# An opening and a first maxout group in one hand-fixed order on every engine, early reads of the second group's blocks, and weights joined in two VectorE operations

## The chip, the cores and the metric

One Trainium2 chip, one core of it. A time is the device time of one execution in microseconds (us), and a kernel's time is the median of its executions in the runs named. All executions told of here were in the fast state, so no slow run had to be set aside. A span is the profiled execution from its first to its last instruction; it is 1 to 3 us shorter than the time.

## The reference, cut to what matters

```python
# delta rule: q, k, v are (4, 8, 768, 48), beta is (4, 8, 768)
k_n = k / (np.linalg.norm(k, axis=-1, keepdims=True) + 1e-06)
for t in range(S):
    y[:, :, t] = einsum('bhd,bhde->bhe', q_t, state)
    v_old      = einsum('bhde,bhd->bhe', state, k_t)
    state      = state + b_t * einsum('bhd,bhe->bhde', k_t, v_t - v_old)
x = y.transpose(0, 2, 1, 3).reshape(3072, 384)
# maxout layer with d_ff = 768
h = np.maximum(np.maximum(x @ w1, x @ w2), x @ w3)
out = h @ w_out
```

The kernel takes the delta rule in chunks of 64 steps, twelve chunks, two to a *group*, six groups. A chunk needs the inverse of a small triangular matrix for every batch and head. Group m's inverses are computed by `solve(m)`: 31 steps of elimination on VectorE, each one multiplication and one subtraction that need the step before. Then come joins and products on TensorE, which end in the group's x, and the maxout layer `ffn(m)` of the group: 6 hidden tiles of 3 products and 2 maxima each (in the first group 9, as three of them are done in two halves), and 4 output tiles.

Some names recur. A *unit* is one chunk for half of the batch, so a group has four. `turn` transposes a unit's k or q, and `gram` forms its products; the one that involves q is then multiplied by a triangular mask (the *mask product*). The other goes to DRAM, and its diagonal blocks are read back by `blocks(m)`; they are what `solve(m)` works on. z, u, y and x are the chain after the solve, in this order, and each needs a product on TensorE and a copy (this y is the delta rule's output; the solve's own result is called y as well, `y_bl` in the lines). The *norm* is the scaling of k to unit length.

## The kernel before: the parts that the argument touches

The solve is a serial chain on VectorE. Each engine works through a queue of its own, and an operation that waits at its head holds what stands behind it (an instance below: a copy that was ready to run stood 7.1 us behind two others).

```python
def solve(m):
    x = xs[m]                               # the blocks, read back from DRAM by blocks(m)
    y = work.tile([128, BL, BL], FP32, name="y_bl", bufs=1)
    nc.gpsimd.memset(y, 0.0)
    norm(bl, ...)                           # sqrt on ACT, five small operations on DVE
    ...
    for j in range(BL - 1):                 # "the loop"
        nc.vector.tensor_tensor(out=t_v, in0=x[...], in1=y[...], op=ALU.mult)
        nc.vector.tensor_tensor(out=y[...], in0=y[...], in1=t_v, op=ALU.subtract)
        yield
    # y goes out to DRAM and comes back transposed, as ut2, t1 and ut
    nc.vector.tensor_copy(x[0:32]...., y[0:32])      # staged in x itself
    nc.scalar.copy(x[32:64]...., y[32:64])
```

A piece of the weights (24 in all) is put together from its two halves over three engines: ACT shifts, VectorE takes a sign off, POOL clamps, VectorE does two more operations, POOL adds. The order of only two engines is fixed by hand, SyncE (which issues transfers) and ScalarE, and in the opening alone; a scheduler orders the rest.

```python
with tc.manual_schedule(engines={SP, Activation}):
    ... loads, turn(0..3), gram(0..3) ...
    blocks(0)
    some(conv, 2)                # two pieces of the weights
    some(solving, 32)            # solve(0)
    ... turn(4..7), gram(4..7) ...
    blocks(1)
    join_z(0); some(conv, 1); join_u(0); old_k(0); old_q(0); new(0); to_y(0); to_x(0)
solving = solve(1)
for m in range(GROUPS):
    for i, _ in enumerate(ffn(m)):      # links of the next group's chain between the tiles
        ...
        if i == SOLVE - 2: blocks(m + 2)
        if i == SOLVE:     solving = solve(m + 2)
```

## Time and profile before

| | before |
|---|---|
| median of 3 runs | 623.84 us |
| span | 622.2 us |
| PE busy, of the span | 544.3 us, 87% |
| DVE, ACT, POOL busy | 51%, 25%, 14% |

The shares of a whole span hide the story; the prediction below cuts the span into stretches. Two waits of TensorE between the end of solve(0) and the first group, 52.4 to 74.3, are worth a look because the argument comes back to them (columns: us in total, times, longest):

```profile
PE p_z L447 <- DMA ut<-y_d: 9.0, 2, 8.5
...
PE p_j L466 <- POOL w_sb L216: 3.3, 1, 3.3
```

The first is the way of y through DRAM. The second is a wait put down to weights: the z products were done, but their copy stood in ScalarE's and VectorE's queues.

### The profile page before, as it was taken

The numbers are of one execution on the slowest core, as the hardware profiler recorded it, in microseconds if no ns is written. First come the engines' busy times: TensorE is split into PE (matmuls) and PEld (weight loads), VectorE is DVE, ScalarE is ACT, GpSimd is POOL, SyncE is SP. The second block draws the span as 40 slices with busy tenths as digits, with TensorE's granted clock in tenths as the row PEclk, the third lists the DMA queues.
The fourth block names the chain that finished last, engine by engine and source line by source line (L and its number), as shares of the span: only waits on it lengthen the run. The fifth ranks groups of instructions, "written<-read, shape, count | busy, mean of one in ns | idle before, by whom it ended". The sixth has DMA issues, their size and how long they took to land.

```text
span 622.2 us, 17590 instructions
## 1 busy us (share of the span) xinstructions
PE 544.3 (87%) x7718; PEld 324.9 (52%) x7718; DVE 317.6 (51%) x748; ACT 153.5 (25%) x255; POOL 87.3 (14%) x123
## 2 busy tenths in 40 slices
PE   5361786676799999999999999999999999999997
PEld 4251675452555554655655545555555555554444
DVE  0797159998364982369722499132596222101110
ACT  4333222323421232221332121432112120110001
POOL 7102204445141002000110000200000100000000
PEclk9656599887799999999999999999999999999999
DMA  9775813553771544352355321542103400020002
GB/s 196 141 162 123 184 34 110 137 112 72 205 124 20 108 99 91 79 95 52 77 111 98 65 52 27 106 91 44 36 1 79 77 2 3 3 49 1 0 0 51
DMA packets 158412, 48.47 MB, mean 78 GB/s; under 512 B 143296, under 2 KB 153344, under 8 KB 158336
## 3 DMA queue, kind: packets, MB, share of 16 engines
q1 hardware_dynamic: 156096, 46.87, 36.3%
q8 instruction: 60, 0.98, 0.7%
q10 hardware_dynamic: 2112, 0.39, 0.4%
q14 instruction: 16, 0.13, 0.1%
q0 software_dynamic: 128, 0.10, 0.1%
HBM read 31.56 MB, written 15.73 MB: 76 GB/s over the span
## 4 chain that ended last, share of the span: by engine, by line
PE 66%; DVE 23%; issue 4%; ACT 2%; DMA 2%; POOL 1%; SPq 0%; POOLq 0%; ACTq 0%; DVEq 0%
PE p_h L591 39%; PE p_o L615 11%; DVE tmp L376 7%; DVE y_bl L382 7%; PE p_t L285 3%; PE p_g L307 3%; PE p_u L516 2%; PE p_s L534 2%; PE p_k L488 2%; PE p_y L551 1%; PE p_q L488 1%; PE p_z L447 1%; DVE h L601 1%; PE p_j L466 1%; DVE mant L208 1%
## 5 line engine op out<-in xcount | busy, mean ns | idle before, releaser
L591 PE MATMUL p_h<-xt,w_sb 128*128 128x512 f32 (+1 forms) x702 | 301.4, 578 | 18.8 <-POOL w_sb L216 7.2
L591 PEld LDWEIGHTS p_h<-xt,w_sb 128*128 128x128 f32 x702 | 131.3, 195 | 145.6 <-issue 117.2
L601 DVE TENSOR_TENSOR h<-h,p_h 128x512 f32<-128x512 f32 (+1 forms) x78 | 50.2, 644 | 148.5 <-PE p_h L591 147.3
L615 PE MATMUL p_o<-wo_sb,h 128*128 128x384 f32 x288 | 96.5, 489 | 1.6 <-DVE h L601 1.5
L615 PEld LDWEIGHTS p_o<-wo_sb,h 128*128 128x128 f32 x288 | 53.6, 190 | 39.7 <-DVE h L601 4.6
L376 DVE TENSOR_TENSOR tmp<-x_bl,y_bl 128x31 f32<-128x31 f32 (+15 forms) x186 | 69.2, 372 | 4.9
L382 DVE TENSOR_TENSOR y_bl<-y_bl,tmp 128x31 f32<-128x31 f32 (+15 forms) x186 | 65.8, 354 | 4.6
L599 ACT COPY h<-p_h 128x512 f32<-128x512 f32 (+1 forms) x39 | 21.6, 553 | 129.7 <-PE p_h L591 129.7
L258 POOL TENSOR_TENSOR v_t<-v_t,nrm 128x768 f32<-128x768 f32 x12 | 17.8, 1482 | 175.1 <-DMA v_t<-in_v_dram 51.1
L307 PE MATMUL p_g<-kqt 64*64 64x64 f32 (+1 forms) x1280 | 33.4, 250 | 8.4 <-ACT kqt L291 7.1
L307 PEld LDWEIGHTS p_g<-kqt 64*64 64x64 f32 x1280 | 28.3, 149 | 16.8 <-ACT kqt L291 10.0
L291 ACT COPY kqt<-p_t 128x1024 f32<-128x1024 f32 (+1 forms) x28 | 24.6, 890 | 28.6 <-PE p_t L285 28.5
L285 PE MATMUL p_t<-ident,kpad 128*128 128x128 f32 x96 | 19.1, 333 | 11.5 <-DMA kpad<-in_k_dram 11.5
L623 ACT COPY o_sb<-p_o 128x384 f32<-128x384 f32 x24 | 11.5, 479 | 67.6 <-PE p_o L615 64.5
L203 POOL TENSOR_SCALAR mant<-mant 128x384 f32<-128x384 f32 x24 | 14.4, 600 | 82.7 <-DVE mant L199 57.7
L540 DVE TENSOR_TENSOR st<-st,p_s 128x768 f32<-128x768 f32 x11 | 10.5, 951 | 28.3 <-PE p_s L534 28.3
L456 POOL COPY ut<-ut 32x512 f32<-32x512 f32 x24 | 14.6, 608 | 72.9 <-DMA ut<-y_d 71.9
L285 PE MATMUL p_t<-ident,qpad 128*128 128x128 f32 x96 | 17.7, 313 | 7.1 <-DMA qpad<-in_q_dram 5.2
L447 PE MATMUL p_z<-ut,at 64*32 64x32 f32 x768 | 10.8, 203 | 14.8 <-DMA ut<-y_d 14.8
L317 DVE TENSOR_TENSOR pt<-p_g,mask 128x512 f32<-128x512 f32 x24 | 16.4, 687 | 11.2 <-PE p_g L307 11.1
L216 POOL TENSOR_TENSOR w_sb<-mant,up 128x384 int32<-128x384 int32 x18 | 18.8, 1045 | 23.9 <-DVE mant L212 12.7
L325 ACT COPY at<-p_g 128x512 f32<-128x512 f32 x24 | 14.0, 585 | 32.1 <-DVE pt L317 26.6
(74 smaller groups left out, 444.6 us busy)
## 6 DMA issues: line engine op xcount, KB each, us to landing
w_bits<-in_moe_w_dram SPq DMA_DIRECT2D x18, 384.0 KB, 4.3
at_d<-at SPq DMA_DIRECT2D x48, 128.0 KB, 3.2
qpad<-in_q_dram SPq DMA_DIRECT2D x48, 96.0 KB, 3.4
v_t<-in_v_dram SPq DMA_DIRECT2D x24, 192.0 KB, 4.3
out_dram<-o_sb SPq DMA_DIRECT2D x48, 96.0 KB, 2.2
kpad<-in_k_dram SPq DMA_DIRECT2D x44, 96.0 KB, 3.1
x_bl<-at_d SPq DMA_DIRECT2D x24, 128.0 KB, 3.1
y_d<-y_bl SPq DMA_DIRECT2D x12, 256.0 KB, 3.5
```

The costliest lines, as they stand in the source:

```text
L216: nc.gpsimd.tensor_tensor(out=dst.bitcast(I32), in0=mant_v.bitcast(I32), in1=up_v, op=ALU.add)
L258: nc.gpsimd.tensor_tensor(out=vts[c], in0=vts[c], in1=nrm[:, :, :, None].to_broadcast([128, 2, H, D]), op=ALU.mult,)
L285: nc.tensor.transpose(p_t[:, i, j * 128 : (j + 1) * 128], src[:, 2 * j : 2 * j + 2], ident,)
L291: nc.scalar.copy(kqt.rearrange("p j b i t -> p i (j b) t")[:, some], p_t.rearrange("p i (x t) -> p i x t", t=C)[:, some],)
L307: nc.tensor.matmul(p_g[rows(bb ^ (g * i)), par, c0 : c0 + C * (1 + whole)], kq[:, 0], kq if whole else kq[:, i],)
L376: nc.vector.tensor_tensor(out=t_v, in0=x[:, j, None, j + 1 :].to_broadcast([128, a, b]), in1=y[:, 0:a, j, None].to_broadcast([128, a, b]), ...
L382: nc.vector.tensor_tensor(out=y[:, 0:a, j + 1 :], in0=y[:, 0:a, j + 1 :], in1=t_v, op=ALU.subtract,)
L488: nc.tensor.matmul(p_b[rows(bb), par, c0 : c0 + D], kqt[g][rows(par), j, bb ^ g, i], st[rows(par), bb ^ g, g, j],)
L591: nc.tensor.matmul(p_h, w_sb[i][:, t, f * 128 : (f + 1) * 128], xt[:, t, lo : lo + w], start=(t == 0), stop=(t == KT - 1),)
L599: nc.scalar.copy(h, p_h)
L601: nc.vector.tensor_tensor(out=h, in0=h, in1=p_h, op=ALU.max)
L615: nc.tensor.matmul(p_o, hs[f][:, i * 128 : (i + 1) * 128], wo_sb[:, f], start=(f == 0), stop=(f == FT - 1),)
```

## The change

Its intent: fix the order of all engines by hand in the opening and the first group; start the first blocks' reads earlier and on two queues; warm TensorE's clock up; move squares, masks and scalings off the critical engines; read the second group's blocks (`blocks(1)`) while the first solve's result is still on its way, so that `solve(1)` has its data when the first group starts; and take one VectorE operation out of every weight piece. The core of the diff, with cuts marked:

```diff
-    with tc.manual_schedule(engines={SP, Activation}):
+    by_hand.enter_context(tc.manual_schedule())          # all engines, to the end of ffn(0)
 # weights
-            nc.scalar.mul(up_v, low, 2.0**-29)
-            nc.vector.tensor_scalar(out=mant_v, in0=high, scalar1=0x7FFFFFFF, op0=bitwise_and)
+            nc.scalar.activation(out=mant_v, in_=high, func=Abs)
 ...                                                     # POOL clamps
+            nc.scalar.mul(up_v, low, 2.0**-29)
+            if waiting: joined(*waiting)                     # a piece's second half one call later
 ...
 # opening
+    busy(8, ident, ident)                                # warm-up products
+        gram(n, (0,), two_queues, nc.vector.tensor_copy) # two_queues = (nc.sync, nc.gpsimd)
+    sums_0 = first_squares(); first_norms(*sums_0)
+    some(conv, 1)
+    blocks(0, two_queues)
+    some(conv, 1)
 ...
+    zeros(st, *ut2, *t1, *ut, *zs)                       # before: at the very start
 ...
+        gram(n, (1,), soft=True)                         # mask product on POOL, not on VectorE
+    some(solving, 31)
+    x_t = next(solving)                                  # y staged in another buffer; blocks(1) here
+    busy(8, ident[0:32], x_t...)
+    for _ in range(3): some(conv, 1); fetch()
+    join_z(0); join_u(0); next(solving)
+    some(conv, 1); ...; new(0); some(conv, 1); to_y(0); to_x(0)
     solving = solve(1)
 # first group: tables say what goes between which products
+    FIRST = {0: "s0", 1: "z1 V3", ..., 30: "K14 n5 p9"}
+    CONVERT = (0, 3, 6, 9, 11, ...);  STEPS = (1, 1, 1, 2, ...)
+        if i == 29: blocks(2)
 # second group
+            if m == 1 and i == 0: solving = solve(2)     # before: inside the first group
```

> **What bounds the kernel now.** I read the page's slices first, then cut the span at the places where the work changes, then asked who TensorE waits for, then read single instructions in order of time.
>
> ```profile
> PE   5361786676799999999999999999999999999997
> ...
> DVE  0797159998364982369722499132596222101110
> ...
> PEclk9656599887799999999999999999999999999999
> ```
>
> A digit is 15.6 us. From the twelfth on TensorE is at 9 and its clock is full; before that it is at half or less, with a clock down to half. So the span splits at about 171 us, and a new order can gain only ahead of that. The cuts: solve(0) starts at 28.7 and ends at 52.4, the first maxout group starts at 74.3, solve(1) ends at 145.5, the second group starts at 213.9, the third at 302.7. Columns: stretch, then length and busy time (with instruction count) of PE, weight load, DVE, ACT, POOL, then clock, DMA share, GB/s.
>
> ```profile
> 0.00:28.70 28.70, 14.05 (x292) 10.58 (x292) 10.91 (x24) 11.06 (x21) 14.38 (x38) 0.85 0.92 175
> 28.70:52.40 23.70, 10.88 (x156) 8.81 (x156) 21.60 (x65) 7.70 (x13) 0.00 (x0) 0.57 0.69 147
> 52.40:74.30 21.90, 9.62 (x295) 8.30 (x295) 9.12 (x23) 7.93 (x11) 9.22 (x11) 0.50 0.68 140
> 74.30:94.90 20.60, 17.44 (x604) 14.25 (x600) 9.49 (x21) 4.81 (x10) 1.89 (x2) 0.91 0.34 74
> 94.90:145.50 50.60, 32.84 (x364) 25.34 (x365) 49.99 (x125) 12.52 (x24) 23.30 (x27) 0.91 0.45 110
> 145.50:171.00 25.50, 18.18 (x444) 12.19 (x443) 11.89 (x23) 11.30 (x17) 7.83 (x11) 0.78 0.69 168
> 171.00:213.90 42.90, 42.90 (x550) 24.87 (x551) 28.77 (x73) 9.42 (x19) 9.21 (x10) 1.00 0.44 83
> 213.90:302.70 88.80, 87.08 (x1291) 50.30 (x1290) 58.54 (x152) 24.23 (x41) 7.85 (x8) 1.00 0.42 82
> ```
>
> Four limits stand one after the other: DMA latency to 28.7; a serial DVE loop to 52.4 (DVE 21.6 of 23.7); a chain of small steps over all engines to 74.3, no engine above 45%; then DVE, 49.99 of 50.6 us, to 145.5. After that TensorE rules. The waits of TensorE up to 172 us name the same things:
>
> ```profile
> PE p_z L447 <- DMA ut<-y_d: 13.4, 3, 8.5
> PE p_t L285 <- DMA kpad<-in_k_dram: 11.5, 4, 4.6
> PE p_h L591 <- POOL w_sb L216: 7.2, 3, 3.8
> ```
>
> Columns: us in total, times, longest. And single instructions (start, duration):
>
> ```profile
> 52.12 0.21 DVE L382 TENSOR_TENSOR y_bl<-y_bl,tmp 128x31 f32<-128x31 f32 x1
> ...
> 121.25 1.01 POOL L216 TENSOR_TENSOR w_sb<-mant,up 128x384 int32<-128x384 int32 x1 [1.55 <-DVE mant L212]
> 121.33 1.15 DVE L199 TENSOR_SCALAR mant<-w_bits 128x384 uint32<-128x384 uint32 x1
> ```
>
> The last line is the one to see: the same DVE operation takes 0.34 us at 53.24, and 1.15 us here, where it starts just after a POOL addition and ends with it.
>
> **What the Trainium skill says.** (1) "TensorE: Matmul & The Clock Gate", Part 1: an idle TensorE runs at half clock and needs about 3.4 us of sustained work to get the full one. The trace agrees: 0.50 in 52.4 to 74.3, 1.00 after 171; four transposes take 1.08 us in the first and 0.6 us warm. (2) "SBUF — State Buffer", section "SBUF: two separate sides": VectorE and GpSimd share a port pair that one of them holds for a whole instruction while the other blocks. The two lines above agree. (3) "DMA: Bandwidth & Descriptors", "Issuing engines are not separate DMA queues": a second issuing engine saves only the issue time. In this trace that time is not small: four reads of the first blocks take 4.25 us on SP. But the only transfers issued by GpSimd (beta) have a median of 5.4 us to landing, against 3.1 for the block reads. (4) "ScalarE: Activation LUTs", "Table sets": cheap functions, abs among them, are in every table set. The trace has one table load (1.28 us, at 3.62), with copy, square and sqrt in use; so I expect Abs on ACT to add none.
>
> **The change part by part.**
>
> *Loads to solve(0).* Before, the last copy of the first products ends at 12.84; its transfer out waits behind others (issues until 15.2), the reads run on one queue from 16.96 to 21.2, and the first use (sqrt of the diagonal) is at 23.94. After: eight warm-up matmuls, copies on DVE beside those on ACT, two issuing queues, and the q loads moved behind. Four transposes and copies shortened by about 0.5 us each give 2 us, two queues another 2 of the 4.25; the GpSimd half lands later (5.4 against 3.1 us) and gives 1 back: 3 us earlier, solve starts at 25.7. The two sums of squares (one 0.54 us reduce lies in the loop) move out of it. But POOL, idle (0.00) in the loop before, now gets two v scalings of 1.48 us and four mask products (estimated 1.3 us from its 1.0 us for 384 columns): 8.2 us, each of which can hold up a loop operation of two SBUF operands. I take a quarter, 2 us. Loop 23.7 - 0.5 + 2 = 25.2: it ends at 51, 1.4 us earlier.
>
> *solve(0) to the first group, 21.9 us before.* Writing y out and reading it back was 52.33 to 57.5, the second half 58.4; it stays, 6 us. Then z waited until 62.07 for squares in the ACT queue: these are gone, about 3 us. The clock is warm: two joins, two products and six transposes of 1.1, 1.1, 2.0, 2.0 and 1.5 us become 0.7, 0.7, 1.1, 1.1 and 0.8: 3.3 us. Three copies of 0.8 us split over two engines save about 0.3 each: 0.9. Given back: DVE and POOL have three weight pieces in their queues ahead of the z copy, and POOL also issues t1 reads there: I take 1.3. So 16 us, and the first group starts at 67.
>
> *First group up to the end of solve(1), 71.2 us before.* x of the second group is there at once, and solve(1) starts at 67; before it did at 89.8 and took 55.7 us. DVE's work in this part: solve 23 + 4 of setup; 13 pieces x (0.35 + 0.55) = 11.7 (before 0.35 more each); maxima 12 x 0.41 + 2 x 0.69 = 6.3; chunk 1 (two st of 0.95, z 0.69, v 0.95, ut 0.69, y 0.95) 5.2; two norms 4.4. Sum 54.7. Instructions ready at once overlap by 0.08 us in the records, some 80 of them: -6. Stretching by POOL: of 23.3 us POOL in the DVE-bound stretch before I count some 11 us as lost to DVE; with one operation less per piece to be hit and a hand order I take 8. So 57 us. TensorE's own work is less: 18 x 1.49 + 3 x 2.68 for the hidden layer, 8.4 for chunk 1, 4.6 for transposes and products: 48. DVE still sets the pace; solve(1) ends at 124.
>
> *Rest of the first group, 68.4 us before.* TensorE: 6 x 2.68 + 4 x 3.9 = 31.7; chunks 2 and 3, 14.9; transposes and products of the third group, 6: 52.6. Latency of y to the second z was 157.2 - 145.5 = 11.7 us, with only some 7 us of matmuls placed before it: 5 us idle. 57.5 us; the second group starts at 181.5 instead of 213.9.
>
> *Second group.* 88.8 before. Two mask products move in (1.1), and solve(2), which had begun at 195, now begins with the group while its z stands after eight steps (26 us of TensorE against some 32 + 6 of chain). The scheduler may fill that, so 2 us in all: 90.8. From the third group on 622.2 - 302.7 = 319.5, unchanged: TensorE is at 86 of 87 to 89 us per group.
>
> Sum: 67 + 57 + 57.5 + 90.8 + 319.5 = 591.8 us of span; the time is 1.6 above the span before (623.84 against 622.2), so **593.4 us**, 4.9% less.
>
> **The rivals.** (A) TensorE-bound first group: the hand order hides all of DVE. The group then takes its matmul work, 48 + 52.6 = 101 us, and the time is 580. For it: 30% fewer DVE instructions per piece; against it: DVE at 49.99 of 50.6, and a queue in order can't slip an operation past a blocked one. (B) Head-of-line waits and POOL: in a fixed order a DVE operation that waits for POOL stops all behind it; with POOL at 8.2 us in the first loop and at some 30 in the group, twice the stretching I took costs 2 + 8 us, and GpSimd-issued transfers on the path 3: 606. For it: the 1.15 us line. (C) The gain moves into the second group: solve(2) late, z waits, TensorE idle by the whole 12 us that I mostly let the scheduler fill: 603. For it: its start moved from the first group into the second; against: all of the group's own matmuls are independent of z. (D) A transfer hides all of the opening's gain: 600.
>
> **Range and chances.** A alone gives 580, with a better opening 576; B and C together come to some 610. So 577 to 608 for 8 in 10. 2% is 611.4: faster by over 2%, 0.93; within, 0.06; slower, 0.01.
>
> **What would show it.** Right: first maxout matmul near 67; the loop of solve(0) some 25 us with POOL busy in it; clock near full from the z join on; DVE nearly full from 67 to 124; an idle stretch of TensorE of some 5 us after solve(1); groups from the third on still 87 to 89 us; one table load. Wrong: a first maxout matmul at 74 (D); DVE with gaps and TensorE full in the first group (A); DVE operations of over 1 us all through (B); idle TensorE in the second group (C).

## The result, and the profile after

The changed kernel takes 657.65 us (median of 4 runs, 655.84 to 659.44) against 623.11 of the kernel before in the same rounds. The ratio is 1.0554, 95% interval 1.0513 to 1.0595: slower, by 5.5%, where 4.9% faster was predicted. Ratios here and below are the mean time of one kernel's fast runs over that of the other's of the same rounds, so not quite the ratio of the medians quoted. The changed kernel is correct.

The same marks as in the prediction, in the profiled executions. A loop is said to start when the last multiplication of its setup ends; where other work comes in between, its first step runs up to 2 us later, and in one run 10 us later, as said there.

| mark (us) | before | predicted | after |
|---|---|---|---|
| loop of solve(0) starts | 28.7 | 25.7 | 32.5 |
| it ends | 52.4 | 51 | 61.0 |
| first maxout product | 74.3 | 67 | 87.4 |
| loop of solve(1) ends | 145.5 | 124 | 165.4 |
| second group starts | 213.9 | 181.5 | 222.4 |
| third group starts | 302.7 | 272.3 | 331.5 |
| end of the span | 622.2 | 591.8 | 654.8 |

The slices after, to lay beside those of before in the prediction (a slice is now 16.4 us):

```profile
PE   5173389655799967989989999899999999999997
...
DVE  3697377977541379433971337942359622201110
...
PEclk9567579988899979999979999999999999999999
```

TensorE's nines no longer begin at the twelfth slice and stay: a dip stands at the 15th and 16th, inside the second group, and the clock falls there and again in the 21st. The stretches (columns as in the prediction: length; busy time and instructions of PE, weight load, DVE, ACT, POOL; clock, DMA share, GB/s):

```profile
0.00:32.60 32.60, 10.81 (x187) 9.32 (x190) 14.93 (x26) 8.65 (x18) 18.85 (x44) 0.70 1.09 185
32.60:61.20 28.60, 14.91 (x292) 11.79 (x287) 26.45 (x63) 10.69 (x16) 6.84 (x5) 0.74 0.40 80
61.20:87.40 26.20, 12.86 (x278) 11.00 (x278) 10.21 (x17) 9.10 (x17) 12.63 (x18) 0.50 0.82 176
87.40:165.40 78.00, 57.89 (x792) 39.96 (x793) 64.28 (x130) 24.70 (x51) 31.80 (x34) 0.87 0.40 96
165.40:222.40 57.00, 52.67 (x1198) 34.38 (x1196) 20.70 (x34) 20.62 (x35) 11.86 (x15) 0.96 0.49 104
222.40:331.50 109.10, 93.93 (x1392) 52.41 (x1386) 70.29 (x181) 26.38 (x48) 9.51 (x9) 0.96 0.36 69
```

Every stretch but the fifth is longer than predicted. In the fourth VectorE is busy for 64.28 of 78 us, so it is not the full engine that the prediction counted on; in the last, TensorE stands idle for 109.10 - 93.93 = 15.2 us. Two waits of TensorE over the whole execution name places:

```profile
PE p_h L663 <- DVE h L674: 23.1, 9, 6.9
...
PE p_j L531 <- ACT z L517: 7.8, 1, 7.8
```

### The profile page after: what moved, and what is told of

The parts are those of the page before. It is cut to its first block, busy times and chain, and to the rows that moved or that the text cites. A ratio compares the mean times of both kernels' runs of the same rounds, so it can differ in the third digit from the quotient of the medians.

```text
span 654.8 us, 17792 instructions
## 1 busy us (share of the span) xinstructions
PE 557.5 (85%) x7818; PEld 330.2 (50%) x7818; DVE 329.0 (50%) x719; ACT 164.5 (25%) x282; POOL 105.1 (16%) x142
## 4 chain that ended last, share of the span: by engine, by line
PE 63%; DVE 17%; issue 4%; DMA 3%; ACT 2%; POOL 1%; SPq 1%; ACTq 0%; DVEq 0%; POOLq 0%
PE p_h L663 37%; PE p_o L688 10%; DVE tmp L429 5%; DVE y_bl L435 5%; PE p_g L353 2%; PE p_u L581 2%; PE p_t L331 2%; PE p_s L599 2%; PE p_k L553 1%; PE p_q L553 1%; PE p_y L616 1%; DVE mant L229 1%; DVE h L674 1%; PE p_z L512 1%; DMA ksum<-kflip 1%
## 5 line engine op out<-in xcount | busy, mean ns | idle before, releaser
L663 PE MATMUL p_h<-xt,w_sb 128*128 128x512 f32 (+1 forms) x702 | 308.6, 589 | 34.9 <-DVE h L674 23.1
L435 DVE TENSOR_TENSOR y_bl<-y_bl,tmp 128x31 f32<-128x31 f32 (+15 forms) x186 | 75.8, 407 | 5.3
L429 DVE TENSOR_TENSOR tmp<-x_bl,y_bl 128x31 f32<-128x31 f32 (+15 forms) x186 | 71.7, 386 | 5.0
L353 PE MATMUL p_g<-kqt 64*64 64x64 f32 (+1 forms) x1344 | 31.5, 238 | 16.8 <-ACT kqt L337 16.8
L353 PEld LDWEIGHTS p_g<-kqt 64*64 64x64 f32 x1344 | 26.7, 142 | 24.4 <-ACT kqt L337 20.3
L337 ACT COPY kqt<-p_t 128x1024 f32<-128x1024 f32 (+1 forms) x28 | 24.5, 889 | 14.6 <-PE p_t L331 14.6
L521 POOL COPY ut<-ut 32x512 f32<-32x512 f32 x24 | 14.6, 608 | 69.9 <-DMA ut<-y_d 68.9
L233 POOL TENSOR_TENSOR w_sb<-mant,up 128x384 int32<-128x384 int32 x18 | 18.9, 1051 | 10.4 <-DVE mant L229 10.4
L621 DVE TENSOR_TENSOR y<-qs,p_y 128x768 f32<-128x768 f32 x11 | 10.5, 951 | 19.5 <-PE p_y L616 19.5
L206 ACT ACTIVATE mant<-w_bits 128x384 f32<-128x384 f32 x24 | 13.2, 549 | 26.7 <-POOL w_sb L233 20.6
L646 ACT COPY u<-p_u 128x768 f32<-128x768 f32 x11 | 8.8, 800 | 39.1 <-PE p_u L581 39.1
L378 ACT COPY at<-p_g 128x512 f32<-128x512 f32 x20 | 11.6, 586 | 27.1 <-DVE pt L370 23.9
L518 DVE COPY z<-p_z 32x512 f32<-32x512 f32 x12 | 8.2, 688 | 20.4 <-ACT z L517 20.3
```

The source lines that it names most:

```text
L233: nc.gpsimd.tensor_tensor(out=dst.bitcast(I32), in0=mant_v.bitcast(I32), in1=up_v, op=ALU.add)
L337: nc.scalar.copy(kqt.rearrange("p j b i t -> p i (j b) t")[:, some], p_t.rearrange("p i (x t) -> p i x t", t=C)[:, some],)
L353: nc.tensor.matmul(p_g[rows(bb ^ (g * i)), par, c0 : c0 + C * (1 + whole)], kq[:, 0], kq if whole else kq[:, i],)
L429: nc.vector.tensor_tensor(out=t_v, in0=x[:, j, None, j + 1 :].to_broadcast([128, a, b]), in1=y[:, 0:a, j, None].to_broadcast([128, a, b]), ...
L435: nc.vector.tensor_tensor(out=y[:, 0:a, j + 1 :], in0=y[:, 0:a, j + 1 :], in1=t_v, op=ALU.subtract,)
L521: nc.gpsimd.tensor_copy(ut[c % NU][low, :, :, BL:C], ut2[c % NU][low])
```

## The experiments

Five causes were on the table after a first reading of the two traces, and most runs test one or two of them:

1. *Zeros.* POOL's memsets, moved to just ahead of the solve, hold VectorE.
2. *Masks.* The mask products, now on POOL, hold the loop of solve(0), and perhaps the group as well.
3. *Weights.* Weight pieces stand ahead of the z copy.
4. *Hand order.* A fixed order on VectorE, POOL and TensorE stops ready work behind work that waits.
5. *solve(2).* It starts late and runs inside the second group.

Each runs against a rival: that the cause is real in the trace but hidden behind something else, so that its removal moves no time. The kernel before measured between 623.2 and 624.5 us in the rounds of all batches, while the four runs of one variant lie up to 6 us apart; differences of medians of 1 or 2 us are not read as effects. The expectations were written batch by batch, each knowing only the runs before it; the changed kernel is called "after" in some. They are told here by cause, not in the order in which they ran.

### Zeros ahead of the solve

These lines of the changed kernel are at the start of solve(0) (start, duration, engine, line, operation, and in square brackets how long the engine had been idle and what ended that):

```profile
24.97 3.04 DVE L241 TENSOR_SCALAR nt_bl<-root_bl 128x32 f32<-128x32 f32 x1 [5.54 <-ACT root_bl L240]
25.65 1.85 POOL L92 MEMSET ut<- 128x1024 f32 x2
27.44 1.02 POOL L92 MEMSET z<- 128x512 f32 x2
...
28.43 1.55 DVE L243 TENSOR_TENSOR nt_bl<-nt_bl,x_bl 128x32 f32<-128x32 f32 x1
28.43 1.46 POOL L272 TENSOR_TENSOR v_t<-v_t,nrm 128x768 f32<-128x768 f32 x1
```

A VectorE operation on 32 elements a partition takes 3.04 us while POOL's memsets run one after another; the same operation takes 0.18 us elsewhere. The second one, 0.21 elsewhere, ends with a scaling of v on POOL. `zeros_early` puts all memsets where they were, at the start, and the loads of beta, which are also issued by POOL, behind the first products (not in the cut):

```diff
+    zeros(*(t[:, :, D:DP] for t in qpad + kpad[4:]))
+    zeros(st, *ut2, *t1, *ut, *zs)
     fetch(); fetch()
 ...
-    zeros(...)   # both calls, between blocks(0) and the loop
```

> One edit to the changed kernel: all memsets stand ahead of the first products in POOL's queue (as before the change), the beta loads behind the first products. Theory P: a DVE operation of 32 columns took 3.04 us (0.18 elsewhere) because POOL's 6.6 us of memsets, back to back, lay on the port just then; and the next one 1.55 against 0.21. The loop of solve(0) then starts at about 29 instead of 32.5, and 3 to 4 us come off the time: 653. Rival (DVE waited for the block data, not for POOL): the loop starts within 1 us of 32.5, 656 to 658.

Measured: 651.79 us, ratio 1.0453 (1.0431 to 1.0475). The two operations are short again,

```profile
24.01 0.18 DVE L241 TENSOR_SCALAR nt_bl<-root_bl 128x32 f32<-128x32 f32 x1 [4.93 <-ACT root_bl L240]
...
24.62 0.21 DVE L243 TENSOR_TENSOR nt_bl<-nt_bl,x_bl 128x32 f32<-128x32 f32 x1
```

the loop starts at 27.4 instead of 32.5, and 5.1 us at the start are worth 5.9 at the end. This cause is shown: 4.2 of the 5.1 us lie between the square root's end and the loop, where the two operations are, and 1.0 in an earlier square root.

It leaves a question: the square root before these lines starts at 24.7 in the changed kernel, and at 23.9 in the kernel before, although SyncE issues the first reads 3.6 us earlier. The other half of the reads is POOL's:

```profile
13.32 1.07 SPq L397 DMA_DIRECT2D x_bl<-at_d  x2
...
17.30 0.50 POOL L210 TENSOR_SCALAR mant<-mant 128x384 f32<-128x384 f32 x1 [4.62 <-ACT mant L206]
17.94 1.82 POOL L397 DMA_DIRECT2D x_bl<-at_d  x2
```

A weight piece stands ahead of the two issues in POOL's queue and waits 4.62 us for ScalarE. The issues then take 1.82 us, and their transfers 5.4 us to landing (SyncE's: 3.0). The longer landing need not be POOL's doing: the writes of at_d just before, which the two engines issue side by side, took 2.9 us from POOL and 3.0 from SyncE, and POOL's late reads fall among the loads of v and q. `zeros_one_queue`, run last of all, is `zeros_early` with the reads on SyncE alone:

```diff
-    blocks(0, two_queues)
+    blocks(0)
```

> Version with all memsets ahead of the loop, and its four reads of the first blocks issued by SyncE alone instead of two by SyncE and two by GpSimd. Theory that the GpSimd half is what is late (it is issued only at 17.3 us, behind a weight piece that waits for ScalarE, and takes 5.4 us to landing against 3.0): SyncE issues all four between about 13.4 and 17.5, the last lands near 20.5, the square root of the diagonal starts at 20 to 21 instead of 23.7, and the loop of solve(0) at 23.5 to 24.5 instead of 27.4; the time 648 to 650 against 651.8. Rival, that the products' writes or the DMA engines themselves gate the reads: the square root stays at 23 to 24 and the loop at 27, the time at 652.

Measured: 651.54 us, ratio 1.044 (1.0397 to 1.0483).

```profile
13.85 3.03 SPq L397 DMA_DIRECT2D x_bl<-at_d  x4
...
20.18 0.26 ACT L240 ACTIVATE root_bl<-x_bl 128x32 f32<-128x32 f32 x1 [1.56 <-DMA x_bl<-at_d]
20.48 1.18 DVE L241 TENSOR_SCALAR nt_bl<-root_bl 128x32 f32<-128x32 f32 x1 [0.89 <-ACT root_bl L240]
20.67 0.95 POOL L414 MEMSET y_bl<- 128x1024 f32 x1
```

The square root comes at 20.2, as the theory had it, so the half on POOL, behind its weight piece, was what was late. But the loop started only at 25.8, not at 24: the memset of y and the v scaling now fall on the small operations. And the time did not move beyond its spread: the first group's first copy came 1.2 us earlier (84.3 against 85.5). This reading of the opening is right, and the time it was said to be worth is not shown.

### Masks on POOL

In the loop of solve(0) of the changed kernel:

```profile
33.96 1.27 POOL L365 TENSOR_TENSOR pt<-pt,mask 128x512 f32<-128x512 f32 x1 [4.07 <-ACT pt L364]
...
34.15 1.22 DVE L429 TENSOR_TENSOR tmp<-x_bl,y_bl 128x112 f32<-128x112 f32 x1
```

A loop operation that takes 0.27 us takes 1.22, to the end of POOL's product. There are four mask products and one v scaling in the loop, and each hits one operation; the excess of the five adds up to 5.05 us. `no_masks` leaves the product out, and so gives a wrong result on purpose:

```diff
                 nc.scalar.copy(by_par(pt), p_v[:, :, :, 1])
-                nc.gpsimd.tensor_tensor(out=pt, in0=pt, in1=mask..., op=ALU.mult)
```

> Wrong result on purpose: POOL's mask product is left out for the first eight units, all else as in the changed kernel. Theory P: the loop of solve(0) loses the four stretches of about 1 us and ends at 57 instead of 61.0; in the first group four more products of 1.4 us, each holding up DVE for about 1 us once or twice, go: solve(1) ends 4 (opening) plus 4 to 6 us earlier, 156 to 158 instead of 165.4; 648 to 651 us. Theory H: only the 4 us of the opening come back, 653 to 655.

Measured: 653.27 us, ratio 1.047 (1.0432 to 1.0508), wrong as intended (relative error 0.268). The loop took 24.6 us instead of 28.5, and the gain is 4.4 us in all. The stretch from the first maxout product on got no shorter, so that the mask products stretched the group as well is not borne out.

`masks_on_dve` gives them back to VectorE, as before the change, in the hand order:

```diff
-        gram(n, (1,), soft=True)
+        gram(n, (1,), soft=False)
```

> One edit to the changed kernel: the eight mask products of the first two unit groups go back from ACT plus POOL to one DVE operation each (0.69 us). Theory P: in the loop of solve(0) four POOL products held up a loop operation by 0.95 to 1.03 us each; taking them out gives 4 us and costs 4 x 0.69 = 2.8; in the first group four more, each of which held up one or two operations by about 1 us, give 5 and cost 2.8: 3 to 4 us faster, 653. Theory H: the masks then stand in DVE's fixed order behind solve steps and wait for TensorE there; no gain or a loss of a few us, 656 to 661.

Measured: 662.03 us, ratio 1.0626 (1.0588 to 1.0665): worse. The setup of the solve ends at 32.5 as before, but the loop's first step runs only at 42.5, and its last ends at 67.0 instead of 61.0:

```profile
41.87 0.69 DVE L370 TENSOR_TENSOR pt<-p_g,mask 128x512 f32<-128x512 f32 x1 [2.16 <-PE p_g L353]
42.48 0.18 DVE L429 TENSOR_TENSOR tmp<-x_bl,y_bl 128x31 f32<-128x31 f32 x1
```

This is the last of the four products. They stand in VectorE's fixed queue ahead of the loop, and the last three wait 2.16 us each for TensorE. The loop itself then takes 24.5 us instead of 28.5. The masks on POOL cost 4.4 us, and in this hand order the way back costs more.

### Weights ahead of the z copy

Between the end of solve(0) and the first group, in the changed kernel:

```profile
66.98 1.07 PE L512 MATMUL p_z<-ut,at 64*32 64x32 f32 x60 [0.58 <-DMA ut<-y_d]
...
74.30 0.54 ACT L206 ACTIVATE mant<-w_bits 128x384 f32<-128x384 f32 x1 [3.31 <-DMA w_bits<-in_moe_w_dram]
74.75 0.53 ACT L215 ACTIVATE up<-w_bits 128x384 int32<-128x384 uint32 x1
...
75.19 0.56 ACT L517 COPY z<-p_z 32x512 f32<-32x512 f32 x1
75.84 0.28 PE L531 MATMUL p_j<-z,t 64*32 64x32 f32 x2 [7.80 <-ACT z L517]
```

The z products are done at 68.05. Their copy is ready to run and stands in ScalarE's queue behind the second and the third weight piece: the second waits for POOL until 70.01, the third for its transfer until 74.30. TensorE waits 7.80 us. `weights_behind` puts the three pieces behind the joins:

```diff
-    for _ in range(3): some(conv, 1); fetch()
     join_z(0); join_u(0); next(solving)
+    for _ in range(3): some(conv, 1); fetch()
```

> One edit to the changed kernel: the three weight pieces between solve(0) and the z join go behind the two joins in program order. Theory H: z was copied at 75.19 although its matmuls ended at 68.05, because ACT's copy stood behind the Abs of a piece that waited for POOL and for a weight load; z is now copied at about 68.2, the first maxout matmul moves from 87.4 to about 80, and the time falls by 6 to 8 us to 650. Rival (the wait only moves: the pieces are needed by the first maxout steps anyway, or t1 arrives late): the first maxout matmul moves by under 3 us, 654 to 657.

Measured: 659.21 us, ratio 1.0568 (1.0533 to 1.0603): no gain. The z copy starts at 68.25, 6.9 us earlier, and then:

```profile
84.23 0.47 ACT L648 COPY u<-p_u 128x384 f32<-128x384 f32 x1
...
84.74 2.54 PE L616 MATMUL p_y<-u,pt 64*64 64x48 f32 x64 [8.25 <-ACT u L648]
```

The wait has moved down the chain, from z to u, and the first maxout product comes at 90.6, not at 80. A guess from this is that the amount of weight work ahead of the first group is what counts, and not its place: the changed kernel calls for seven pieces there, the kernel before for four. `fewer_weights` below tests it.

### The hand order on VectorE, POOL and TensorE

In the first group of the changed kernel, around TensorE's longest wait for a maximum, VectorE ran these two, one after the other:

```profile
161.06 0.68 DVE L674 TENSOR_TENSOR h<-h,p_h 128x512 f32<-128x512 f32 x1
161.66 0.35 DVE L225 TENSOR_SCALAR mant<-mant 128x384 uint32<-128x384 uint32 x1
```

and TensorE these:

```profile
149.78 5.18 PE L663 MATMUL p_h<-xt,w_sb 128*128 128x512 f32 x11
161.89 5.23 PE L663 MATMUL p_h<-xt,w_sb 128*128 128x512 f32 x6 [6.93 <-DVE h L674]
```

The products were done at 154.96, and their maximum, 0.68 us of work, ran at 161.06: between them the fixed queue of VectorE held five pairs of solve operations and the two of a weight piece. TensorE waited 17.6 us for maxima between 87.4 and 165.4. In the same stretch VectorE itself stood for 13.7 us; 11.1 of them are waits that the profile names, and 6.1 of these, in two pieces, are at the norm's small operations, whose sums were still on their way through a transfer. `free_order` leaves SyncE and ScalarE in the hand order and gives the rest back to the scheduler:

```diff
-    by_hand.enter_context(tc.manual_schedule())
+    by_hand.enter_context(tc.manual_schedule(engines={SP, Activation}))
```

> One edit to the changed kernel: only SP and ACT keep the hand order up to the second group; PE, DVE and POOL are ordered by the scheduler again, as they were before. Theory H (a queue in fixed order: an operation that waits holds up what stands behind it): the 17.6 us that TensorE waits for maxima in the first group shrink by half or more, and the loop of solve(1), which ends at 165.4, ends 10 to 15 us earlier; 640 to 646 us. Theory P (the placing of work: POOL's mask products and memsets lock the port that DVE needs, whatever the order): the same instructions still collide, 652 to 660 us. The second group, which was never in hand order, stays near 109 us by both.

Measured: 659.71 us, ratio 1.058 (1.0551 to 1.0608): not better. From the first copy of the first group to its end it took 120.5 us instead of 131.9, so the group did gain its 11 us. But what follows the loop of solve(0) came late. The loop was over at 54.2, and ScalarE's half of the copy after it started at 74.0, where it had started at 61.0: the scheduler had put the second warm-up's products, which wait for the staged y, in between other products on TensorE, and TensorE and with it ScalarE stood until the loop was over:

```profile
55.30 0.79 PE L726 MATMUL p_w<-xt,ident 32*128 32x128 f32 x2 [17.52 <-DVE xt L458]
56.02 1.13 PE L357 MATMUL p_g<-kqt 64*64 64x64 f32 x32
```

`free_no_warm` takes that second warm-up out as well:

```diff
-    busy(8, ident[0:32], x_t...)
```

> The free order of DVE, POOL and PE again, without the eight warm-up matmuls on x_t, which the scheduler had put between the products of the second unit group, so that these waited for the end of solve(0) (TensorE and ACT stood from 38.4 to 57). Theory H in its second form (the fixed order costs in the first group, where the free run needed 120.5 us from its first maxout step to the group's end against 132 in hand order): with the opening mended the time is 657.7 less about 11 in the group and 5 in the opening: 640 to 644. If the free order loses in the opening what it gains in the group: 652 to 660.

Measured: 644.39 us, ratio 1.034 (1.0317 to 1.0363), 13.3 us better. The scheduler also started the memsets earlier (the loop starts at 27.5), so some 5 of this are the zeros' part. The loop of solve(1) ends 43.9 us after the first maxout product instead of 78 (130.2 against 86.3), with VectorE busy for 40.4 of the 43.9 us; the scheduler leaves other work of VectorE for later. The group as a whole gains less, 124.5 us instead of 135.0 from its first product to the next group's. What follows the loop is the work of the two engines that keep the hand order: SyncE writes y out from 153.2, ScalarE's half of the copy starts at 155.1, and so the result stands for 23 us (in `repairs_free` below for 21). In the changed kernel both follow the loop at once. The hand order of these three engines is a loss here, and the warm-up is one in the free order; the hand order without the second warm-up was not run.

### solve(2) inside the second group

In the changed kernel the third group's blocks are read at the end of the first group, and then:

```profile
219.60 3.10 SPq L397 DMA_DIRECT2D x_bl<-at_d  x4
...
230.94 1.93 ACT L337 COPY kqt<-p_t 128x1024 f32<-128x1024 f32 x2 [2.82 <-PE p_t L331]
...
232.75 0.27 ACT L240 ACTIVATE root_bl<-x_bl 128x32 f32<-128x32 f32 x1
233.05 0.18 DVE L241 TENSOR_SCALAR nt_bl<-root_bl 128x32 f32<-128x32 f32 x1 [5.39 <-ACT root_bl L240]
```

The loop runs from 236.4 to 266.8, in the second group, where the kernel before had it from 200.9 to 228.7. Two runs move it. `solve2_early` takes the read and the start of the solve one to two tiles forward:

```diff
-        if i == 29: blocks(2)
+        if i == 28: blocks(2)
+        if i == 30: solving = solve(2); some(solving, 9)
```

> One edit to the changed kernel: the blocks of the third group are read one step earlier and solve(2) starts with nine steps in the last step of the first group instead of in the second group. Theory L (solve(2) late makes DVE the bound of the second group's start, 109.1 us against 88.8 before): the loop starts some 6 us earlier and ends before z is due; the second group takes 98 to 102 us and the time falls by 7 to 10 us to 648. Rival (the second group is slow because of its new links and mask products, not because of solve(2)): within 3 us of the changed kernel, 654 to 657.

Measured: 651.14 us, ratio 1.0445 (1.0411 to 1.0479), 6.5 us better, with the loop from 227.7. `solve2_earlier` reorders the first group's table so that the third group's products and norms come sooner (11: "k2 q2", 13: "t8", 16: "t10 a8", ..., 20: "a11"), reads the blocks at i = 22 and starts the solve at i = 25. It also splits the squares of two norms of the first group from the rest of them, so that VectorE need not stand for their sums, and from then on gives four steps of the solve to each tile.

> The changed kernel with the list of the first group's links put in another order: chunk 2's products with the state right after chunk 1, the third unit group's transposes and products at steps 13 to 20 instead of 15 to 27, its blocks read at step 22, solve(2) from step 25 on with four steps each; and the squares of n2 and n3 split from their norms, so that DVE's queue does not stand for the 3 us of the row sums' transfer. Theory L: the loop of solve(2) starts at about 195 to 200 as before the change; the second group takes 92 instead of 105 us and the third 86 instead of 94: 635 to 640 us. Rival (the group's links, not solve(2)): 648 to 652 as with the first, weaker form.

Measured: 638.06 us, ratio 1.024 (1.0204 to 1.0277), 19.6 us better: the largest gain of a single run. The loop starts at 195.5, and the second group up to its last output copy:

```profile
220.30:317.20 96.90, 91.42 (x1354) 51.73 (x1346) 57.65 (x140) 25.18 (x44) 9.29 (x9) 0.96 0.36 69
```

The same stretch of the changed kernel, 222.4 to 327.5, takes 105.1 us, so this is 8.2 us less. TensorE is idle for 5.5 us in it instead of 12.7, and VectorE is 8.9 us less loaded, as part of the solve's steps have left it (the loop still runs to 240.4). Counted to the next group's first product, as in the table of marks, the second group takes 98.9 us instead of 109.1. In the profiled executions the second group ends 10.3 us earlier than in the changed kernel (317.2 against 327.5), the third 15.2 (406.1 against 421.3), and that stays to the end; this profiled execution was the slowest of the four (641.4 us), so the medians differ by more. As the run changes several things, it doesn't show how much of its gain is due to the start of solve(2) alone.

### The repairs together, and each part alone

`repairs_fixed` keeps the hand order: `solve2_earlier` with `zeros_early`.

> The changed kernel in its hand order with both repairs that worked: memsets early (651.8 alone) and the third unit group and solve(2) earlier (638.1 alone). If the two losses are independent, as their places in the span say, 638.1 - 5.9 = 632. If the second repair has eaten slack that the first needs, 635 to 638.

Measured: 630.86 us, ratio 1.0135 (1.0102 to 1.0168). `repairs_free` is `solve2_earlier` with `free_no_warm`.

> Free order of PE, DVE and POOL (644.4 alone; the scheduler also puts the memsets early) with the earlier solve(2). Additive: 644.4 - 18 = 626, within 1% of the kernel before. Theory H then leaves nothing of the 33 us to explain but the opening's ACT queue. If it stays above 632, something else in the change costs.

Measured: 627.44 us, ratio 1.007 (1.0054 to 1.0087). The parts measured alone add up to 657.65 - 5.9 - 19.6 = 632.2 us for the first and 657.65 - 13.3 - 19.6 = 624.8 for the second, so they are nearly additive: 30.2 of the 34.5 us lost are found. But they only bring the time back to that of the kernel before. The profiled executions show where the expected gain went (us from the first maxout product of a group to that of the next):

| stretch | before | changed | `repairs_free` |
|---|---|---|---|
| up to the first maxout product | 74.3 | 87.4 | 85.0 |
| first group | 139.9 | 135.0 | 123.2 |
| second group | 88.3 | 109.1 | 96.1 |
| from the third group on | 319.6 | 323.3 | 320.4 |

In `repairs_free` the first group is 16.7 us shorter than in the kernel before, and an opening that is 10.7 us longer and a second group that is 7.8 us longer take that away again. `no_hand_order` frees SyncE and ScalarE as well (`repairs_free` without any manual schedule):

> As the run before, but ACT and SP are free too: nothing of the hand order is left, the program order and the new work placement stay. Theory H on ACT (z copied 7 us late behind the weights' Abs, in the opening) says that the first maxout step moves from about 88 to about 80 and the time is 616 to 620. If the scheduler puts loads in a worse order on SP, 626 or more.

Measured: 645.66 us, ratio 1.0369 (1.0339 to 1.04). The loop of solve(0) starts at 42.3. The first copies on ScalarE come at 14.0 (6.6 in the changed kernel), because the scheduler put squares and two weight pieces ahead of them:

```profile
11.01 0.54 ACT L205 ACTIVATE mant<-w_bits 128x384 f32<-128x384 f32 x1 [3.57 <-DMA w_bits<-in_moe_w_dram]
...
13.98 1.06 ACT L336 COPY kqt<-p_t 128x512 f32<-128x512 f32 x2
```

So the first blocks are written from 21.8 (8.7) and their reads are issued from 26.6 (13.3). A hand order of SyncE and ScalarE together is worth 18 us here, and in the opening the delay is ScalarE's. `before_two_ops` is the kernel before with nothing but the new weights:

```diff
-            nc.vector.tensor_scalar(..., 0x7FFFFFFF, op0=bitwise_and)     # on VectorE
+            nc.scalar.activation(..., func=Abs)                           # on ScalarE
 ...
+            if waiting: joined(*waiting)                                  # a piece's second half one call later
```

> The kernel before with one part of the change alone: Abs of the weights on ACT, two VectorE operations a piece, the second half of a piece issued after the first half of the next. Everything else, the scheduler's order too, as before. If the weights' third DVE operation was worth what the prediction gave it (13 pieces x 0.35 us in the stretch where DVE is the bound, and fewer collisions with POOL), solve(1) ends 4 to 8 us sooner and the time is 616 to 620. If a piece's chain (Abs, POOL, DVE, POOL) and not DVE's count sets the pace, it stays within 2 us of 623.5.

Measured: 628.14 us, ratio 1.0065 (1.0031 to 1.0098), a little slower. One VectorE operation of three less per piece wins nothing; solve(1) ends 3.9 us earlier (141.7) and solve(2) 1.6 later (230.3). Profiled, the first group is 3.3 us shorter than in the kernel before, and the second 5.6 us longer (93.9); why, no run shows.

### Looking for the missing gain in the tables and the weights

Four more runs on top of `repairs_free`. `old_table` restores the kernel before's order for the later groups:

```diff
-    LINKS = {0: "k0 q0", 2: "t0 t1", 7: "z0 z1 t2", ...};  SOLVE = 17
+    LINKS = {0: "k0 q0", 1: "t0 t1", 2: "g0 g1", 3: "z0 z1 t2", ...};  SOLVE = 12
```

> repairs_free (627.4) with the links, the start of the solves and the loads of the second to the last group in the old order (z at step 3, the next solve from step 12, the last transpose two steps before the group's end). If the new order of these groups costs (repairs_free is 2.0, 3.7, 1.2, 0.1 and 1.8 us per group behind the kernel before from the second on), the sum of some 7 to 8 us comes back: 619 to 621. If those differences come from the chip's clock or from loads, not from the order, 626 to 628.

Measured: 630.47 us, ratio 1.0136 (1.0097 to 1.0175): not better. `fewer_weights` leaves two pieces instead of five between solve(0) and the first group, and puts the others into the group:

```diff
-    for _ in range(3): some(conv, 1); fetch()
+    some(conv, 1); fetch(); fetch()
     join_z(0); ...
-    CONVERT = (0, 3, 6, 9, ...)
+    CONVERT = (0, 1, 2, 3, 4, 6, 9, ...)
```

> repairs_free (627.4) with one weight piece instead of three between solve(0) and the z copy, none behind the joins, and the three at steps 1, 2 and 4 of the first group. Theory H on ACT: the z copy no longer stands behind an Abs that waits for POOL: it runs at about 62.7 instead of 69.8, the first maxout step moves 6 to 7 us forward. If the group then has DVE time for the three pieces, 620 to 622; if DVE is the bound of the group and the pieces only move (weights_behind moved them by a few us and gained nothing), 626 to 629.

Measured: 627.27 us, ratio 1.0092 (1.0044 to 1.014), the same as `repairs_free`. The first copy of the group comes 4 us earlier (83.8 against 87.8), and the group ends 0.7 later (208.8 against 208.1). The weights are paid for either here or there. `table_weights` is both:

> Both edits of the two runs before it. Additive: 627.4 - 7 - 6 = 614, faster than the kernel before by 1.5%.

Measured: 630.48 us, ratio 1.0101 (1.0063 to 1.0139). `table_weights_masks` has the masks on VectorE in addition:

> The run before it with the eight mask products as one DVE operation each. In the free order a mask need not stand ahead of the loop (in hand order it did: solve(0) ended 6.0 us later): three POOL products in the loop of solve(0) gone give 3 us against 4 x 0.69 = 2.8 spent: 612 to 615, no gain by either theory unless POOL's products cost more in the group than they did in no_masks (nothing there).

Measured: 638.55 us, ratio 1.0265 (1.0229 to 1.0302), 8.1 us worse than without them. The loop of solve(0) itself ends earlier, at 52.9 instead of 55.1. But the scheduler put the fourth mask product behind the loop, at 53.83; TensorE waited 10.0 us for it, and with the products behind it the queue of ScalarE, whose half of the copy of y started at 67.9 instead of 55.1. So even where the scheduler orders VectorE, masks there delay the way from the solve to the group. None of these is faster than the kernel before. What all have in common is that solve(1) starts with the first group, at 84 to 98 us.

### One part alone: the second solve as soon as its blocks are there

The last theory: the early read was hardly used. In the changed kernel all blocks of the second group are there at 73.2 (the last read of them is issued at 68.9), but the code starts `solve(1)` after `to_x(0)`, with the first group, and its loop starts at 90.6; in the kernel before it started at 94.6. Nor was the read any earlier on the clock, as the loop of solve(0) ended 8.6 us later. The kernel before and the changed one:

```profile
65.95 3.60 SPq L344 DMA_DIRECT2D x_bl<-at_d  x4
...
89.80 0.26 ACT L224 ACTIVATE root_bl<-x_bl 128x32 f32<-128x32 f32 x1
```

```profile
66.49 3.35 SPq L397 DMA_DIRECT2D x_bl<-at_d  x4
...
86.66 0.26 ACT L240 ACTIVATE root_bl<-x_bl 128x32 f32<-128x32 f32 x1
```

In both, the square root that begins the setup of solve(1) comes 18 to 21 us after the last read was issued. What the change did reach is that solve(1) begins with the first group and not 15.5 us into it. Everything that delays the chain from solve(0) to the first group also delays solve(1), whose result the second group's chain needs. In the kernel before, VectorE is busy for 9.12 of the 21.9 us ahead of the first group. `before_solve1_early` is the kernel before with the part of the change that reads `blocks(1)` early (with the other staging buffer that it needs), and with something that the change does not have, the start of `solve(1)` and ten steps of it moved up to just behind the first joins:

```diff
 # in solve's tail
+        if m == 0: x_t = ...              # y staged in another buffer than x
 ...
+            if m == 0 and cc == 0: blocks(1)
 # opening
-        blocks(1)
         join_u(0)
+        solving = solve(1)
+        some(solving, 1)
         old_k(0); old_q(0); new(0)
+        some(solving, 10)
```

> The kernel before with one part of the change taken further: the transposed copy of solve(0)'s result goes to another buffer, the second group's blocks are read at once, and solve(1) is started right after the first joins (in the changed kernel it starts only at the first maxout step). DVE is 42% busy from 52 to 74 us, so some ten of the 31 steps fit in there. solve(1) then ends at 115 to 125 instead of 145.5; of the 18 us for which TensorE idles in 94.9 to 145.5, half come back: 610 to 616. Rival (the weight pieces, not solve(1), set that stretch; DVE has the same total to do): within 3 us of 623.

Measured: 607.79 us, ratio 0.9729 (0.9685 to 0.9774), correct: 2.7% faster than the kernel before and the best of all kernels here. The square root of the second solve's diagonal now starts at 66.5 (86.7 in the changed kernel),

```profile
66.52 0.26 ACT L224 ACTIVATE root_bl<-x_bl 128x32 f32<-128x32 f32 x1 [1.14 <-DMA x_bl<-at_d]
```

and the stretches from the end of solve(0) to the first group, and from there to the end of solve(1):

```profile
52.50:75.60 23.10, 9.39 (x294) 8.16 (x294) 17.05 (x48) 8.26 (x13) 9.22 (x11) 0.50 0.65 136
75.60:111.85 36.25, 28.67 (x684) 22.45 (x681) 34.25 (x86) 9.25 (x20) 12.24 (x15) 0.86 0.52 130
```

The loop of solve(1) starts at 70.7 instead of 94.6 and ends at 111.9 instead of 145.6. Ahead of the first group VectorE is busy for 17.05 us instead of 9.12, with work that delays the group's start by only 1.5 us (its first copy at 78.8 instead of 77.3). The first group's last output is copied at 198.7 instead of 214.9, and the 16 us stay to the end. The reads are now issued 5 us earlier than in the kernel before (from 60.99), and the loop starts 23.9 us earlier. The early start without the early read was not run, and neither was this start in the changed kernel or in `repairs_free`.

## Why the prediction was wrong, point by point

The prediction missed the span by 654.8 - 591.8 = 63.0 us. Its terms, each against what it measured:

| term | predicted | measured | missed by |
|---|---|---|---|
| start of the loop of solve(0) | 25.7 | 32.5 | 6.8 |
| the loop | 25.2 | 28.5 | 3.3 |
| solve(0) to the first group | 16 | 26.4 | 10.4 |
| first group to the end of solve(1) | 57 | 78.0 | 21.0 |
| rest of the first group | 57.5 | 57.0 | -0.5 |
| second group | 90.8 | 109.1 | 18.3 |
| from the third group on | 319.5 | 323.3 | 3.8 |

The last column adds up to the miss, but for rounding.

**The step that failed most** is "DVE still sets the pace; solve(1) ends at 124". It sums VectorE's work, 54.7 us, takes 6 for overlap, adds 8 for stretching by POOL, and sets the stretch's length to that sum, as if no operation would ever have to wait. VectorE's busy time was indeed larger (64.28), 7.6 us of the 21; the other 13.7 are VectorE idle, 11.1 of them in waits of the operation at the head of its queue. The kernel before had DVE at 49.99 of 50.6 there, and that was a scheduler's order. The prediction named this ("Head-of-line waits and POOL") but gave it, as rival B, 8 us for the group, and called the hand order an argument for less stretching. `free_no_warm` shows it the other way round: in the scheduler's order VectorE is busy for 40.4 of the 43.9 us up to the end of solve(1), and that end comes 35 us earlier.

**"Two in all" for the second group** failed by 18.3 us. The prediction saw that z would stand after eight steps against a chain of some 38 us, and trusted that "the scheduler may fill that"; rival C, the same in its full size, was put at 12 us. It missed that the solve could not start with the group: its blocks are read from 219.6, its square root waits in ScalarE's queue to 232.75, and its loop starts 14 us into the group. `solve2_earlier`, which moves this start together with its unit group's links, is worth 19.6 us. In its profile the second group is 10.2 us shorter (98.9), the first 2.2, and the rest 2.9. The other 8 us by which the second group exceeds 90.8 stay open.

**Solve(0) to the first group.** Writing y out and reading it back took 5.1 us (5.2 before), as said. Two terms failed. "The clock is warm", 3.3 us: the clock was 0.50 over this whole stretch although the eight warm-up products ran. "I take 1.3" for weights in the queue: the z copy waited 7.1 us after its products, where it had waited 2.6 before. 3.3 and some 6 make up most of the 10.4.

**Loads to solve(0).** The copies on VectorE and the earlier first issues came true (13.3 us instead of 16.96). "The GpSimd half lands later and gives 1 back" was too small: it was issued behind a weight piece and took all of the 3 us (`zeros_one_queue`: the square root at 20.2 without it). The reason given, beta's 5.4 us to landing, was no measure for it: other writes that both engines issued side by side landed alike (2.9 and 3.0 us). And the memsets moved by the diff were not looked at: 5.1 us (`zeros_early`).

**The loop.** "I take a quarter, 2 us" of POOL's 8.2 us: the excess was 5.05. The mechanism, one of two engines waiting for the other's whole instruction, was right and the share was too low: each of the five POOL operations in the loop hit one of VectorE's.

**Right:** the rest of the first group, 57.5 against 57.0; Abs added no second table load (one, at 3.62 us, as before); and that TensorE's part from the third group on is out of reach, which missed by 3.8 us; 2.9 of these lie in the third group (91.9 us instead of 88.9) and are gone in `solve2_earlier` and in `free_no_warm` (320.4 us each from the third group on).

**Slips that change nothing.** VectorE's work in the first group adds up to 54.6, not 54.7. The four transposes of 1.08 us are not in the stretch 52.4 to 74.3 but at 4.6 us; in that stretch six took 1.54. Only one of the two v scalings fell into the loop.

**What tied it together:** the prediction gave the early read its value through "solve(1) starts at 67". It was to start with the first group, and so every us lost in front of the group held solve(1) up as well: it started at 86.7. That early read and early start together are worth something is shown by `before_solve1_early`; that this change used little of it is shown by the 90.6 us at which its loop started, 4.0 before that of the kernel before.

What stays open: `repairs_free` loses 10.7 us in the opening and 7.8 in the second group against the kernel before. It still carries the masks on POOL (4.4 us in the changed kernel) and the long weight chain, and no run shows what each of them costs there. The order of links in the later groups is not the reason for the second group's 96.1 us: with the old one, in `old_table`, it takes 96.1 as well.

## What to carry to other kernels

A sum of an engine's busy times is the length of a stretch only while something fills its queue around every wait; when a change fixes that queue by hand, count for each operation what can be late in front of it, transfers above all. When a change brings data earlier, look for the instruction that uses it: here an early read with an early start of the second solve won 2.7%, and a rewritten opening that read at the same time and started the solve later lost 5.5%. And an idle engine is not a free one: work moved to POOL took 5.05 us from VectorE's loop.

## What the Trainium skill lacked or had wrong

- "SBUF — State Buffer", "SBUF: two separate sides": it has the shared port pair held for a whole instruction. The mask products agree (0.27 us became 1.22). It does not say that the waiting side can stand through several instructions of the other: one VectorE operation of 0.18 us took 3.04 us during a run of POOL memsets of 0.5 to 0.9 us each, and 0.18 us when `zeros_early` had moved them.
- "TensorE: Matmul & The Clock Gate", Part 1: some 3.4 us of sustained work for the full clock. 3.78 us of back-to-back products in the opening were followed by four transposes in 0.66 us (7.86 us; the same take 1.09 without the warm-up, at 6.30 in the kernel before); 3.78 us of products on 32 partitions after solve(0) were followed by 60 z products in 1.07 us (0.72 warm, at 275.97) and a clock of 0.50 up to 87.4 us. So 3.78 us are not always enough. The page itself has the clock's window run freely, which would allow for that; whether it is this or the 32 partitions, no run here shows.
- "DMA: Bandwidth & Descriptors", "Issuing engines are not separate DMA queues": it counts the saved issue time only, and says nothing of what an issue stands behind. Here GpSimd's two issues stood 4.62 us behind a compute operation in GpSimd's own queue, and with all four reads on SyncE the data were there 3.5 us earlier (square root at 20.18 instead of 23.72). As for the transfers, the runs agree with it: writes that both engines issued side by side took 2.9 us (GpSimd) and 3.0 us (SyncE) to landing.
